# Backward pass of a linear-attention and SwiGLU block: the gradient of w2 computed transposed, with hh as the moving operand

## The chip, the cores and the metric

The kernel runs on one NeuronCore of a Trainium2 chip. A NeuronCore has five engines that run side by side and meet only at semaphores: TensorE (matrix multiply, PE in the profile), VectorE (DVE), ScalarE (ACT), GpSimd (POOL) and SyncE (SP), and 16 DMA engines that move data between HBM and the on-chip memory SBUF. A matmul takes a stationary operand (`lhsT`, at most 128 x 128, loaded into the array by a weight load, PEld in the profile) and streams a moving operand (`rhs`) through it; the result is summed in PSUM, whose banks hold 512 float32 values in each of 128 partitions. The metric is device time in microseconds (us).

## The reference

The program is one transformer block, forward and backward, on 2048 tokens of width D = 640: layernorm, linear attention with 32 heads of 20, a residual; then layernorm, a gated MLP with F = 1728 hidden columns, a residual. All arrays are bfloat16. The outputs are the block's output and the gradients of its input and of the five weights. The part that matters here:

```python
def _B_ref(x, w1, w3, w2):
    gate = jnp.einsum("bsd,df->bsf", x, w1)
    up = jnp.einsum("bsd,df->bsf", x, w3)
    h = _silu(gate) * up
    out = jnp.einsum("bsf,fd->bsd", h, w2)
    return out
...
h2 = h + _B_ref(_layernorm(h, axis=-1), B_w1, B_w3, B_w2)
...
_out, _vjp = jax.vjp(_f, A_x, A_wqkv, A_wo, B_w1, B_w3, B_w2)
_grads = _vjp(grad_out)
```

The gradient of w2, [1728, 640], is hidden^T times grad_out: for each hidden column f and each model column d, the sum over the 2048 tokens of h[s, f] x grad_out[s, d]. In the kernel it is `out_6`. The gradients of w1 and w3, [640, 1728] each, are `out_4` and `out_5`.

## The kernel before

The kernel is written with a manual schedule: the order of the code is the order of each engine's instructions, and of the DMA queues that SP, ACT and GpSimd issue into. The framework adds the waits: a reader waits for its writer, and a tile that takes over another's memory waits for its last user. `dma` is a copy issued from SP, `dmaT` a transposing load issued from SP, `dmaG` a copy issued from GpSimd, `A.dma_start` a copy issued from ACT. An engine that issues a DMA waits, in its queue, for what that DMA needs; what stands behind it waits too.

The stages in time (us from the start of the span):

1. Up to about 343: layernorms, the forward attention and the MLP. The MLP runs over four chunks of 512 tokens and 14 tiles of 128 hidden columns (the last has 64); the hidden activations are written to HBM transposed, as `hh_d` [F, S], and what the backward pass of w1 and w3 needs as `gg_d` [2F, S]. The last of it on TensorE is the down projection of the last chunk (`o2_steps`, lines 849 and 878).
2. 343 to 402, the gradient of w2 (lines 1033 to 1103). `load_hh` (line 1035) brings back `hh_d` with transposing loads, in four blocks of hidden columns of 512, 512, 512 and 192, as `hb[b]` [128 tokens of a tile, 16 tiles, columns]; block 0 comes in two loads of 256. Block 3 takes the buffer of block 0 (tags "ABCA"). `g2` holds grad_out by tokens. For each of 13 full tiles `fc` of 128 hidden columns, and each half j of D (320 columns), 16 matmuls sum over the token tiles: the stationary operand is 128 columns of hh, the moving operand 320 columns of `g2` (line 1089). ACT casts the two halves (line 1092), and issues the write of the 128 x 640 tile to `out_6` (line 1093). The last 64 hidden columns are `gw2_tail` (line 1070), called before the last full tile: 32 matmuls with a stationary operand of 64 columns, the two halves of D at two halves of the array. Between the tiles SP is given the loads that come next: block 3 of hh after fc 3, the transposed w1 and w3 (`load_w13`, line 1057) after fc 5, the first two pieces of `gg_d` (`load_gg`, line 1064) after fc 8 and 11.
3. 402 to 564: the gradient at the second layernorm (`b_ghn`, line 1126, with 27 x 2 matmuls a token tile), then the gradients through the output projection and the heads. The tile `g_h` [128, 16 token tiles, 640] is written here, and used up to the last token tile of stage 5.
4. 564 to 628: gradients of the attention's products, and of wqkv.
5. 628 to 702: the gradient at the first layernorm, by token tiles (`e_gxn`, line 1502). In it SP loads the first two blocks of `gg_d` (`load_block`, line 1478), again transposing, 496 columns of the 3456 (2F) a block, into two alternating buffers `gb`.
6. 702 to the end (lines 1540 to 1554): the gradients of w1 and w3. For each of seven blocks and each of five slices m of D, `grad_job` (line 1328) runs 16 matmuls with 128 columns of the normalized activations `hnN` as the stationary and up to 496 columns of `gb` as the moving operand (line 1338), with eight accumulators; ACT casts the result into `obs` (line 1342) and issues the write (line 1344), in halves for the first four jobs. SP first transposes the gradient of wo (kept in HBM as `dwoT_d`) into the first five tiles of `g_h`, which are free by then (line 1543), and writes it out (line 1544); then, after the jobs of block i, it loads block i + 2, whose buffer is block i's.

Of the kernel before, what the change touches and what calls it, by code (L numbers as in the profile page):

```python
# [9 lines left out]
P = 128  # L10
BF16 = mybir.dt.bfloat16
F32 = mybir.dt.float32
# [6 lines left out]
S, D, H, F = 2048, 640, 32, 1728  # L19
DH = D // H  # L20
ST, DT = S // P, D // P
FT, FP = 14, 1792
FL = F - 13 * P
W, SC, TPC = 512, 4, 4
HD = D // 2
NG = 27
# [29 lines left out]
def kernel(  # L56
# [19 lines left out]
    V, A, T, G, SY = nc.vector, nc.scalar, nc.tensor, nc.gpsimd, nc.sync  # L76
    dma, dmaT, dmaG = SY.dma_start, SY.dma_start_transpose, G.dma_start
# [12 lines left out]
    dram = ctx.enter_context(tc.tile_pool(name="dram", bufs=1, space=bass.MemoryType.DRAM))  # L90
# [5 lines left out]
    w_d = dram.tile([D, D], BF16, name="w_d")  # L96
    kvT_d = dram.tile([D, D], BF16, name="kvT_d")
    dwoT_d = dram.tile([D, D], BF16, name="dwoT_d")
    hn_d = dram.tile([S, D], BF16, name="hn_d")
    hh_d = dram.tile([F, S], BF16, name="hh_d")  # L100
    gg_d = dram.tile([2 * F, S], BF16, name="gg_d")
# [2 lines left out]
    def pool(name, side="left", space=None):  # L104
        kw = dict(space=space) if space is not None else dict(side=side)
        return tc.alloc_tile_pool(name=name, bufs=1, reuse_waits="tile", **kw)
# [71 lines left out]
    ps = pool("p1p", space=PSUM)  # L178
# [48 lines left out]
    def load_w13(c0, c1):  # L227
        def go1():
            dma(out=w1[:, c0:c1, 0:F], in_=rows(B_w1)[:, c0:c1, :])

        def go3():
            dma(out=w3[:, c0:c1, :], in_=rows(B_w3)[:, c0:c1, 0:F - FL])
        return [go1, go3]
# [18 lines left out]
    def p1_tr(t, parts=((0, DT),)):  # L252
        xn = x_sb[:, t, :]
        for a, b in parts:
            tr = ps.tile([P, DT, P], BF16, name="tr", bufs=2)
            for c in range(a, b):
                T.transpose(tr[:, c, :], xn[:, c * P:(c + 1) * P], ident[:])

            A.copy(out=pqT[:, a:b, t * P:(t + 1) * P], in_=tr[:, a:b, :])
# [13 lines left out]
    def p1_mm(t, n0, between=None, halves=None):  # L273
        acc = p1_acc() if halves is None else None
        for j in range(2):
            p1_half(acc[:, j, 0:HD] if halves is None else halves[j][:, 0:HD], t, n0 + j * HD)
            if j == 0 and between is not None:
                between()
        return acc
# [240 lines left out]
    for t in range(ST):  # L520
        first = None
        if t < RAW:
# [11 lines left out]
            k = p1_mm(t, D, between, kh)  # L534
            act(0, 1)
            act(1, 1)
        else:
            k = p1_mm(t, D, (lambda: p1_tr(t + 1)) if t + 1 < XT_DMA else None)
# [95 lines left out]
    ps = pool("pap", space=PSUM)  # L634
# [350 lines left out]
    for c in range(SC):  # L985
# [9 lines left out]
        for fc in range(FT):  # L995
# [8 lines left out]
            if c == 0 and fc in (5, 7, 9, 11):  # L1004
                a, b = {5: (0, 3), 7: (3, 6), 9: (6, 10), 11: (10, 13)}[fc]
# [10 lines left out]
            if c == SC - 1 and fc == 0:  # L1016
                g2 = U1.tile([P, ST, D], BF16, name="g2", tag="Q")
                tail = U2.tile([P, DT, P], BF16, name="w13tail", tag="g2T", bufs=2)
            if c == SC - 1 and fc in (1, 2, 5, 6):
                i = (1, 2, 5, 6).index(fc)  # L1020
# [9 lines left out]
    drain(1)  # L1030


    hb, blk = {}, [(0, 512), (512, 512), (1024, 512), (1536, 192)]

    def load_hh(b):
        f0, fw = blk[b]
        hb[b] = U2.tile([P, ST, 512], BF16, name="hb", tag="ABCA"[b])
        for a, n in ((0, 2 * P), (2 * P, 2 * P)) if b == 0 else ((0, fw),):
            dmaT(out=hb[b][:, :, a:a + n], in_=hh_d[f0 + a:f0 + a + n, :])

    load_hh(0)
    for _ in o2_steps(SC - 1, A.dma_start):
        drain(1)
# [6 lines left out]
    br = pool("br", "right")  # L1050
    ps = pool("pcp", space=PSUM)
    load_hh(1)
    load_hh(2)
    woT = U1.tile([P, DT, D], BF16, name="woT", tag="W6")
    kvN = br.tile([P, DT, D], BF16, name="kvN")
# [8 lines left out]
    def load_gg(j, c0, c1, q=dma):  # L1064
        if c0 == 0:
            ggb[j] = ba.tile([P, NG, 2 * P], BF16, name="ggb", bufs=2)
        q(out=ggb[j][:, c0:c1, :],
            in_=gg_d[c0 * P:c1 * P, j * 2 * P:(j + 1) * 2 * P].rearrange("(c p) w -> p c w", p=P))

    def gw2_tail():  # L1070

        gt = ps.tile([P, 2, 512], F32, name="gt", tag="gw", bufs=4)
        for t in range(ST):
            for j in range(2):
                T.matmul(gt[j * FL:(j + 1) * FL, 0, 0:HD], lhsT=hb[3][:, t, P:P + FL],
                         rhs=g2[:, t, j * HD:(j + 1) * HD], start=(t == 0), stop=(t == ST - 1))
        ob = br.tile([P, HD], BF16, name="gts")
        A.copy(out=ob[:], in_=gt[:, 0, 0:HD])
        for j in range(2):
            A.dma_start(out=out_6[F - FL:F, j * HD:(j + 1) * HD], in_=ob[j * FL:(j + 1) * FL, :])  # L1080

    for fc in range(FT - 1):
        b, i = divmod(fc, 4)
        if fc == FT - 2:
            gw2_tail()
        acc = ps.tile([P, 2, 512], F32, name="gw", bufs=4)
        for j in range(2):
            for t in range(ST):
                T.matmul(acc[:, j, 0:HD], lhsT=hb[b][:, t, i * P:(i + 1) * P], rhs=g2[:, t, j * HD:(j + 1) * HD],  # L1089
                         start=(t == 0), stop=(t == ST - 1))  # L1090
        ob = br.tile([P, D], BF16, name="gw2o", bufs=2)
        A.copy(out=ob[:].rearrange("p (j n) -> p j n", j=2), in_=acc[:, :, 0:HD])
        A.dma_start(out=out_6[fc * P:(fc + 1) * P, :], in_=ob[:])
        if fc == 3:
            load_hh(3)
        if fc == 5:
            load_w13()
        if fc == 8:
            load_gg(0, 0, NG)
        if fc == 11:  # L1100
            load_gg(1, 0, NG)
    ps.release()
    U2.release()

# [4 lines left out]
    g_h, g_n = g_hx[:, :, G0:G0 + D], g_hx[:, :, G0 + D:]  # L1109
# [4 lines left out]
    ps = pool("pbp", space=PSUM)  # L1114
# [134 lines left out]
    for t in range(ST):  # L1249
# [14 lines left out]
        if t >= 1:  # L1264
# [3 lines left out]
            if t <= 2 * DT:  # L1268
                n = (t - 1) % DT
# [24 lines left out]
    a, b = ST - 1, ST - 2  # L1294
# [33 lines left out]
    def grad_job(lhs, m, rhs, n, out, q=dma):  # L1328
        for _ in grad_halves(lhs, m, rhs, n, out, q):
            pass  # L1330
# [30 lines left out]
    ps = pool("pdp", space=PSUM)  # L1361
# [3 lines left out]
    def d_acc():  # L1365
        return ps.tile([P, 2, 512], F32, name="dkv", bufs=3)

    def square(lhsT, rhs, i):

        acc = d_acc()  # L1370
        for c, a, b, bank, off, first in SQ:
            T.matmul(acc[:, bank, off:off + (b - a) * DH], lhsT=lhsT[:, c, i * P:(i + 1) * P],
                     rhs=rhs[:, c, a * DH:b * DH], start=first, stop=True, skip_group_check=True)
        return acc
# [12 lines left out]
    for m, (a, b) in enumerate(M_H):  # L1387
        n = (b - a) * DH
        acc = ps.tile([P, 512], F32, name="gkvT", tag="dkv", bufs=3)
        for c in range(DT):  # L1390
            T.matmul(acc[:, 0:n], lhsT=woT[:, c, m * P:(m + 1) * P], rhs=QT[:, c, a * DH:b * DH], start=(c == 0),
                     stop=(c == DT - 1))
# [38 lines left out]
    acc = d_acc()  # L1431
    for m in range(DT):
        T.matmul(acc[:, m // 4, m % 4 * P:(m % 4 + 1) * P], lhsT=ones[:], rhs=gzd[:, m, :], start=(m % 4 == 0),
                 stop=True, skip_group_check=True)
# [3 lines left out]
    for t in range(ST):  # L1438
        c, i = divmod(t, TPC)
        u = t // 2  # L1440
        acc = d_acc()
        for j in range(2):
            for k in range(DT):
                T.matmul(acc[:, j, 0:HD], lhsT=xnT[c][:, k, i * P:(i + 1) * P], rhs=gm[:, k, j * HD:(j + 1) * HD],  # L1444
                         start=(k == 0), stop=(k == DT - 1))
# [7 lines left out]
        if t in (2, 5, 8, 11, 14):  # L1453
            n = t // 3
            acc = square(mN, gkv_b, n)
            k = (4, 0, 1, 2, 3)[n]
            ob = obs[:, k * D:(k + 1) * D]
# [6 lines left out]
        if t in (6, 8, 10, 12):  # L1464
            n = t // 2 - 3
# [12 lines left out]
    def load_block(i, a=0, b=NB):  # L1478
        if i < len(blocks):
            f0, f1 = blocks[i]  # L1480
            if a == 0:
                gb[i] = ex.tile([P, ST, NB], BF16, name="gb", bufs=2)
            b = min(b, f1 - f0)
            dmaT(out=gb[i][:, :, a:b], in_=gg_d[f0 + a:f0 + b, :])

    def both_grads(m, f0, f1):

        return [(max(f0, lo) - f0, min(f1, lo + F) - f0, out[:, m, max(f0, lo) - lo:min(f1, lo + F) - lo])
                for lo, out in ((0, out4S), (F, out5S)) if max(f0, lo) < min(f1, lo + F)]
# [24 lines left out]
    ps = pool("pep", space=PSUM)  # L1514
# [26 lines left out]
    ps = pool("pfp", space=PSUM)  # L1541
    njob = 8
    dmaT(out=g_h[:, 0:DT, :], in_=dwoT_d[:, :])
    dma(out=out3S, in_=g_h[:, 0:DT, :])
    for i, (f0, f1) in enumerate(blocks):
        n = f1 - f0
        for m in range(DT):
            last = (i, m) == (len(blocks) - 1, DT - 1)
            for a, b in ((0, n - P), (n - P, n)) if last else ((0, n),):
                c = (a + b) // 2  # L1550
                halves = ((a, c), (c, b)) if i * DT + m < 4 else ((a, b),)
                out = [(x + y - a, z + y - a, to) for y, w in halves for x, z, to in both_grads(m, f0 + y, f0 + w)]
                grad_job(hnN, m, lambda t: gb[i][:, t, a:b], b - a, out, A.dma_start)
        load_block(i + 2)
    ps.release()
    ex.release()
    bv.release()
# [33 lines left out]
```

## Time and profile before

| | |
|---|---|
| median of the 3 runs shown | 822.33 us (821.93 to 822.73) |
| the profiled execution | 823.24 us, of which the span is 821.5 |
| mean granted clock of TensorE | 0.999 of full speed |
| ScalarE, VectorE, GpSimd busy | 39%, 55%, 16% of the span |
| stage 2, the matmuls of line 1089 | 416 of 128x320, weights 128 x 128 |
| stage 2, the casts of line 1092 | 13, 692 ns each |
| stage 2, writes of `out_6` from ACT | 13 of 160 KB, 5.7 us to land (median), and 2 of 40 KB |
| stage 2, loads of hh | 5, 6.9 to 13.4 us to land |
| stage 6, loads of `gb` | 9, 4.8 to 12.3 us to land |
| stage 6, casts of 496 columns | 30, 571 ns each |

How to read it. The span is the time from the first to the last instruction of one profiled execution; the execution's own time has 1.74 us more around it. Times of lines are microseconds from the span's start. The busy time of a matmul overlaps that of the next, so what a stream of matmuls costs is read from the chain of work in order of time, where a piece has a start, a length, a line and a count. Lines marked SPq or ACTq are the instructions that issue DMAs: their length is the time the issuing took; "to landing" counts from the start of the issue until the data is there. In the page's second part each digit is the busy share of a fortieth of the span, in tenths.

### The profile page before, as it was taken

What the parts mean: (1) busy time and instruction counts of PE and PEld (TensorE: products, weight loads), DVE (VectorE), ACT (ScalarE), POOL (GpSimd) and SP (SyncE); (2) the same over time, 40 slices, a digit from 0 to 9 for tenths busy, and PEclk for the clock granted to TensorE, in tenths of its full rate; (3) what the DMA queues carried; (4) which work ended last, traced back from release to release, by engine and by line L of the source; (5) the groups of instructions that cost most, each with busy time, mean ns of one, the idle gap of its engine ahead of it and who ended that gap; (6) DMA issues with size and microseconds to landing.
All of it is one profiled execution on the core that took longest, in us unless ns stands there. A gap on an engine that the chain in (4) does not pass through costs nothing.

```text
span 821.5 us, 13988 instructions
## 1 busy us (share of the span) xinstructions
PE 812.4 (99%) x5427; PEld 513.4 (62%) x5454; DVE 453.0 (55%) x975; ACT 323.2 (39%) x603; POOL 130.8 (16%) x193
## 2 busy tenths in 40 slices
PE   8999999999999999999999999999999999999998
PEld 5677544555555545777777777777777777544444
DVE  7859897999898566400057777772681545200000
ACT  6866687655655666011121212222212334211111
POOL 2234343333323212100001111110220000000000
PEclk9999999999999999999999999999999999999999
DMA  9899989796485556999878897259995797968651
GB/s 248 225 284 229 201 235 286 240 241 165 131 218 158 153 195 168 222 260 249 236 167 183 200 209 191 68 112 178 260 225 93 178 190 165 234 164 184 165 139 36
DMA packets 323745, 157.88 MB, mean 192 GB/s; under 512 B 242528, under 2 KB 316928, under 8 KB 323680
## 3 DMA queue, kind: packets, MB, share of 16 engines
q1 hardware_dynamic: 281056, 116.18, 61.9%
q0 software_dynamic: 7328, 24.48, 8.7%
q10 hardware_dynamic: 35296, 16.34, 8.6%
q8 instruction: 42, 0.69, 0.4%
q14 instruction: 23, 0.19, 0.1%
HBM read 47.09 MB, written 51.13 MB: 120 GB/s over the span
## 4 chain that ended last, share of the span: by engine, by line
PE 96%; DMA 2%; SPq 1%; ACT 0%; DVE 0%; issue 0%
PE mm L387 20%; PE job L1338 19%; PE ghn L1134 14%; PE gxn L1507 8%; PE gw L1089 7%; PE o L903 4%; PE big L267 4%; PE o L849 3%; PE gwo L1222 3%; PE macc L422 3%; PE gr L1191 3%; PE dkv L1444 3%; PE at L647 2%; PE mm L267 1%; DMA g2T<-in_grad_out_dram 1%; DMA pqT<-pql 1%
## 5 line engine op out<-in xcount | busy, mean ns | idle before, releaser
L1338 PE MATMUL job<-gb,hnN 128*128 128x496 bf16 (+3 forms) x576 | 116.8, 366 | 0.0
L1134 PEld LDWEIGHTS <-ggb 128*128 128x128 bf16 x864 | 84.5, 98 | 32.8
L387 PE MATMUL mm<-pqT,w 128*128 128x512 bf16 x396 | 93.3, 379 | 0.9 <-ACT up L793 0.2
L1338 PEld LDWEIGHTS <-hnN 128*128 128x128 bf16 x576 | 55.8, 98 | 61.0
L387 PEld LDWEIGHTS <-w 128*128 128x128 bf16 x540 | 52.7, 98 | 63.6 <-issue 1.4
L1342 ACT CAST obs<-job 128x496 bf16<-128x496 f32 (+4 forms) x56 | 28.5, 509 | 123.7 <-PE job L1338 120.9
L1134 PE MATMUL ghn<-w13a,ggb 128*128 128x320 bf16 x448 | 63.5, 299 | 0.0
L1149 DVE SCALAR_TENSOR_TENSOR wb<-gs,hnb 128x640 f32<-128x640 bf16 x16 | 13.2, 825 | 89.4 <-ACT gs L1146 89.4
L1134 PE MATMUL ghn<-w13b,ggb 128*128 128x320 bf16 x416 | 61.4, 299 | 0.0
L387 PE MATMUL mm<-g2T,w2T 128*128 128x512 bf16 x228 | 58.8, 379 | 0.6
L1089 PE MATMUL gw<-g,hb 128*128 128x320 bf16 x416 | 56.8, 299 | 0.0
L1199 POOL TENSOR_TENSOR sz<-Zb,g_h 128x640 f32<-128x640 bf16 x16 | 20.2, 1260 | 197.7 <-DVE g_h L1200 197.7
L1089 PEld LDWEIGHTS <-hb 128*128 128x128 bf16 x416 | 40.6, 98 | 16.0 <-issue 0.3
L412 ACT CAST ghh<-mm 128x512 bf16<-128x512 f32 x48 | 28.1, 586 | 49.9 <-PE mm L387 41.2
L786 ACT ACTIVATE sig<-mm 128x512 bf16<-128x512 f32 x56 | 33.8, 603 | 24.3 <-PE mm L387 20.6
L1146 ACT ACTIVATE gs<-ghn 128x640 bf16<-128x640 f32 x16 | 11.2, 703 | 78.8 <-PE ghn L1134 78.8
L387 PEld LDWEIGHTS <-w2T 128*128 128x128 bf16 x260 | 25.4, 98 | 24.6 <-issue 1.2
L267 PEld LDWEIGHTS <-pqT 128*128 128x128 bf16 x320 | 30.6, 98 | 14.0 <-issue 1.3
L267 PE MATMUL big<-wqkv,pqT 128*128 128x320 bf16 x250 | 38.4, 299 | 0.2
L822 DVE TENSOR_TENSOR gate<-gate,sig 128x1024 bf16<-128x1024 bf16 x28 | 19.3, 689 | 34.4 <-ACT gate L797 31.6
L1338 PEld LDWEIGHTS <-g 128*128 128x128 bf16 x320 | 31.0, 98 | 11.6
L903 PE MATMUL o<-w,hhT 128*128 128x320 bf16 x224 | 35.0, 299 | 0.0
(216 smaller groups left out, 1368.7 us busy)
## 6 DMA issues: line engine op xcount, KB each, us to landing
hh_d<-hhT SPq DMA_DIRECT2D x24, 256.0 KB, 2.6
gg_d<-gate POOLq DMA_DIRECT2D x24, 256.0 KB, 4.1
gg_d<-ghh POOLq DMA_DIRECT2D x24, 256.0 KB, 4.1
ggb<-gg_d SPq DMA_DIRECT2D x6, 896.0 KB, 5.3
ggb<-gg_d ACTq DMA_DIRECT2D x6, 832.0 KB, 6.3
x_sb<-in_A_x_dram SPq DMA_DIRECT2D x6, 640.0 KB, 5.8
ggb<-gg_d SPq DMA_DIRECT2D x2, 1728.0 KB, 13.2
out_dram<-obs ACTq DMA_DIRECT2D x21, 124.0 KB, 3.1
```

The costliest lines, as they stand in the source:

```text
L267: T.matmul(acc, lhsT=pqT[:, c, t * P:(t + 1) * P], rhs=wqkv[:, c, n0:n0 + HD], start=(c == 0), stop=(c == DT - 1))
L387: T.matmul(acc[:], lhsT=w[:, c, fc * P:(fc + 1) * P], rhs=rhs[:, c, :], start=(c == 0), stop=(c == DT - 1))
L412: A.copy(out=ghh[n // 2][:, n % 2, :], in_=acc[:])
L422: T.matmul(macc[m][j][:, 0:n], lhsT=pk_all[:, t, m * P:(m + 1) * P], rhs=x_ext[:, t, j * HD:j * HD + n], start=(t == 0), stop=(t == ST - 1))
L786: A.activation(sig[:, i, :], gp[:], AF.Sigmoid)
L849: T.matmul(accs[i, j][:, 0:HD], lhsT=hhT[c][:, fc, i * P:(i + 1) * P], rhs=w2[:, fc, j * HD:(j + 1) * HD], start=(first and fc == 0), stop ...
L903: T.matmul(o2["ps"][:, 0:HD], lhsT=hhT[c][:, fc, i * P:(i + 1) * P], rhs=w2[:, fc, j * HD:(j + 1) * HD], start=(fc == 0), stop=(fc == FT - 1))
L1089: T.matmul(acc[:, j, 0:HD], lhsT=hb[b][:, t, i * P:(i + 1) * P], rhs=g2[:, t, j * HD:(j + 1) * HD], start=(t == 0), stop=(t == ST - 1))
L1134: T.matmul(acc[:, j, 0:HD], lhsT=ggb[t // 2][:, k, lo:lo + P], rhs=rhs[:, j * HD:(j + 1) * HD], start=(k == 0), stop=(k == NG - 1))
L1338: T.matmul(acc[:, 0:n], lhsT=lhs[:, t, m * P:(m + 1) * P], rhs=rhs(t), start=(t == 0), stop=(t == ST - 1))
L1342: A.copy(out=ob, in_=acc[:, 0:n])
L1507: T.matmul(acc[:, j, 0:HD], lhsT=g, rhs=wqT[:, k, j * HD:(j + 1) * HD], start=(k == 0), stop=(k == 14))
```

## The change

The gradient of w2 is computed as its transpose, [640, 1728]. For each block of hidden columns, now 256, 512, 512 and 448 wide, and each of the five slices of 128 columns of D, 16 matmuls have the slice of `g2` as the stationary and the whole block of hh as the moving operand. The separate tail is gone. A result is one PSUM bank (eight of them instead of four pairs); ACT casts it into one of three buffers and writes it to a new array in HBM, `gw2T_d` [640, 1792]; the last block is padded to 512 columns with zeros by GpSimd. The loads that were issued between the tiles are issued after the blocks: block 3 of hh after block 0, w1 and w3 after block 1, the pieces of `gg_d` after blocks 2 and 3. Block 0 is loaded by one transposing load of 256 columns.

In the last stage SP issues four transposing loads of `gw2T_d` into free tiles of `g_h` (tiles 5 and 6, 7 to 10, 11 to 14, and 0 to 3 once the gradient of wo has been written out from there), two before the jobs of block 0 and two behind the load of block 2; and, behind the load of block 3, the five copies from there to `out_6`. The first seven jobs instead of four write their results in halves.

```diff
+    gw2T_d = dram.tile([D, FP], BF16, name="gw2T_d")
...
-    hb, blk = {}, [(0, 512), (512, 512), (1024, 512), (1536, 192)]
+    hb, blk = {}, [(0, 256), (256, 512), (768, 512), (1280, 448)]
 
     def load_hh(b):
         f0, fw = blk[b]
         hb[b] = U2.tile([P, ST, 512], BF16, name="hb", tag="ABCA"[b])
-        for a, n in ((0, 2 * P), (2 * P, 2 * P)) if b == 0 else ((0, fw),):
-            dmaT(out=hb[b][:, :, a:a + n], in_=hh_d[f0 + a:f0 + a + n, :])
+        dmaT(out=hb[b][:, :, 0:fw], in_=hh_d[f0:f0 + fw, :])
...
-    def gw2_tail():
-
-        gt = ps.tile([P, 2, 512], F32, name="gt", tag="gw", bufs=4)
-        for t in range(ST):
-            for j in range(2):
-                T.matmul(gt[j * FL:(j + 1) * FL, 0, 0:HD], lhsT=hb[3][:, t, P:P + FL],
-                         rhs=g2[:, t, j * HD:(j + 1) * HD], start=(t == 0), stop=(t == ST - 1))
-        ob = br.tile([P, HD], BF16, name="gts")
-        A.copy(out=ob[:], in_=gt[:, 0, 0:HD])
-        for j in range(2):
-            A.dma_start(out=out_6[F - FL:F, j * HD:(j + 1) * HD], in_=ob[j * FL:(j + 1) * FL, :])
-
-    for fc in range(FT - 1):
-        b, i = divmod(fc, 4)
-        if fc == FT - 2:
-            gw2_tail()
-        acc = ps.tile([P, 2, 512], F32, name="gw", bufs=4)
-        for j in range(2):
+    for b, (f0, fw) in enumerate(blk):
+        for m in range(DT):
+            acc = ps.tile([P, 512], F32, name="gw", bufs=8)
             for t in range(ST):
-                T.matmul(acc[:, j, 0:HD], lhsT=hb[b][:, t, i * P:(i + 1) * P], rhs=g2[:, t, j * HD:(j + 1) * HD],
-                         start=(t == 0), stop=(t == ST - 1))
-        ob = br.tile([P, D], BF16, name="gw2o", bufs=2)
-        A.copy(out=ob[:].rearrange("p (j n) -> p j n", j=2), in_=acc[:, :, 0:HD])
-        A.dma_start(out=out_6[fc * P:(fc + 1) * P, :], in_=ob[:])
-        if fc == 3:
+                T.matmul(acc[:, 0:fw], lhsT=g2[:, t, m * P:(m + 1) * P], rhs=hb[b][:, t, 0:fw], start=(t == 0),
+                         stop=(t == ST - 1))
+            ob, fp = br.tile([P, 512], BF16, name="gw2o", bufs=3), (fw + P - 1) // P * P
+            if fp > fw:
+                G.memset(ob[:, fw:fp], 0.0)
+            A.copy(out=ob[:, 0:fw], in_=acc[:, 0:fw])
+            A.dma_start(out=gw2T_d[m * P:(m + 1) * P, f0:f0 + fp], in_=ob[:, 0:fp])
+        if b == 0:
             load_hh(3)
-        if fc == 5:
+        if b == 1:
             load_w13()
-        if fc == 8:
-            load_gg(0, 0, NG)
-        if fc == 11:
-            load_gg(1, 0, NG)
+        if b > 1:
+            load_gg(b - 2, 0, NG)
...
     dmaT(out=g_h[:, 0:DT, :], in_=dwoT_d[:, :])
     dma(out=out3S, in_=g_h[:, 0:DT, :])
+    turned = [DT, DT + 2, DT + 6, 0]
+
+    def gw2_turn(b):
+        f0, fw = blk[b]
+        n = (fw + P - 1) // P
+        dmaT(out=g_h[:, turned[b]:turned[b] + n, :], in_=gw2T_d[:, f0:f0 + n * P])
+
+    def gw2_out(b):
+        f0, fw = blk[b]
+        n, k = fw // P, turned[b]
+        dma(out=out_6[f0:f0 + n * P, :].rearrange("(k p) d -> p k d", p=P), in_=g_h[:, k:k + n, :])
+        if fw % P:
+            dma(out=out_6[f0 + n * P:f0 + fw, :], in_=g_h[0:fw % P, k + n, :])
+
+    for b in range(2):
+        gw2_turn(b)
     for i, (f0, f1) in enumerate(blocks):
...
-                halves = ((a, c), (c, b)) if i * DT + m < 4 else ((a, b),)
+                halves = ((a, c), (c, b)) if i * DT + m < 7 else ((a, b),)
...
         load_block(i + 2)
+        if i == 0:
+            gw2_turn(2)
+            gw2_turn(3)
+        if i == 1:
+            for b in range(4):
+                gw2_out(b)
```

## The prediction, made before the change was run

> **What bounds the kernel now.** I read the page's shares first, then the chain of work that ended last in order of time, then the queue on SP (the engine that issues nearly all loads) in the two stages the change touches. From the page (slices are 20.5 us each):
>
> ```profile
> span 821.5 us, 13988 instructions
> PE 812.4 (99%) x5427; PEld 513.4 (62%) x5454; DVE 453.0 (55%) x975; ACT 323.2 (39%) x603; POOL 130.8 (16%) x193
> DMA  9899989796485556999878897259995797968651
> ```
>
> TensorE is busy 99% of the span, so only fewer or cheaper matmuls, or a shorter tail, can make the kernel faster, and any new wait of TensorE makes it slower by its whole length. DMA is near full in the changed stage (slices 17 to 20) and less full in the last one (35 to 40). The chain in order of time (start, length, what):
>
> ```profile
> 293.46 6.47 PE mm L387 x30
> ...
> 342.88 52.16 PE gw L1089 x384
> 395.04 2.29 PE gt L1075 x32
> 397.34 4.45 PE gw L1089 x32
> 401.79 19.56 PE ghn L1134 x144
> ...
> 568.25 1.56 PE gkvT L1391 x25
> ...
> 701.84 116.65 PE job L1338 x576
> ```
>
> The gradient of w2 is the piece from 342.88 to 401.79, 58.91 us, with no wait inside it or at its ends. The last stage is 116.65 us of matmuls, also unbroken. So both stages are bound by the stream of matmuls, and the loads are hidden. The question is whether they stay hidden.
>
> **What the matmuls cost.** A busy figure of one matmul overlaps its neighbours, so I take spacings from the chain: 52.16/384 = 135.83 ns for 320 columns, 6.47/30 = 215.67 ns for 512 (line 387). That is 0.4158 ns a column and 2.76 ns fixed. A test: 496 columns give 209.0 ns, and a block of the last stage takes (735.34 - 718.61)/80 = 209.1 ns. Before: 416 of 320 columns, plus 32 tail matmuls that run two at a time, 58.91 us in sum. After: 80 matmuls (5 slices of D, 16 token tiles) of 256, 512, 512 and 448 columns: 80 x (109.2 + 215.67 + 215.67 + 189.05) ns = 58.37 us. The columns streamed are the same (13 x 2 x 16 x 320, with half of 32 x 320 for the tail, is 138,240, as is 80 x 1728). What is saved is the fixed part of 128 matmuls and the tail's pairs: **0.54 us**. The 256-column width has no row. The 140-column row (line 1391) takes 62.4 ns where the formula gives 61.0, with a new weight load for each, so 256 columns cost 109.2 to 110.6 ns: at most 0.1 us for the 80. I take the low end, as 320 columns lie nearer.
>
> The Trainium skill, "TensorE: Matmul & The Clock Gate", section "Back-to-back issue gap", gives sustained spacings of about 131 ns at 512 columns and 81 at 128, and says that the columns-plus-fixed formula counts too much at large widths. By a line through its two figures the stage would be about 9 us shorter, an estimate from that page. This trace has 215.67 ns at 512 columns, so I don't use it.
>
> **ScalarE, GpSimd and the stage's end.** 13 casts of 692 ns and one of 425 become 20, of 256 to 512 columns (586 ns is the row for 512). Groups end every 1.75 us at the soonest. A write of 160 KB took 5.7 us to land; with three output buffers a cast in the 256-column block may wait up to 5.7 - 3 x 1.75 = 0.5 us. Behind it in ACT's queue stand only this stage's casts and writes, and TensorE has eight accumulators (14 us of work in that block), so it waits for none. The five small memsets are on GpSimd, which has nothing between 335 and 410. The next stage takes over banks whose casts are long done, save the last, which it needs only at its second tile 8.7 us later. All this: nothing. Without that cover, 0.5 us a cast.
>
> The Trainium skill, "DMA: Bandwidth & Descriptors", section "Bandwidth", calls transfers under 64 KB dominated by their descriptors; that speaks against pieces of 64 KB as the first block writes. Here 62 KB writes from ACT took 3.1 us in the median and 124 KB ones 3.0 to 3.2 in the same busy stretch, so halving brings nothing back. By the rule the five first writes would cost as much as large ones; nobody waits for them.
>
> **The loads of hh, the tight place.** SP in the changed stage:
>
> ```profile
> 331.85 33.91 SPq L1039 DMA_TRANSPOSE hb<-hh_d  x5
> 365.81 9.18 SPq L1058 DMA_TRANSPOSE w13a<-in_B_w_dram  x1
> 375.21 10.41 SPq L1059 DMA_TRANSPOSE w13b<-in_B_w_dram  x1
> 387.25 4.63 SPq L1067 DMA_DIRECT2D ggb<-gg_d  x2
> ```
>
> It issues one load behind the other. Asked one by one, the hb loads land like this (rows of hh; issue; landing): 256 at 331.85 and 340.65; 256 at 336.88 and 346.9; 512 at 343.39 and 354.5; 512 at 351.90 and 365.3; 192 at 362.14 and 369.0. After, the pieces are 256, 512, 512, 448, the same 1728 rows. The first lands as before. The second is needed when the 256-column block is done: 342.88 + 80 x 0.1092 = 351.62. Before, 512 rows had landed by 346.9 and 1024 by 354.5, so 768 are there at about 350.7; ACT's 64 KB writes begin at 344.6 instead of 348 and may add 0.3. It is in time by 0.6 to 0.9 us. Bounds: issued at 336.88 and as quick as the 343.39 load, 11.1 us, it lands at 348.0; the 6.51 us issue of the second 256 rows, then a whole 10.0 us issue and 3.8 us to land, give 357.2. I take 351, nearest to the row counts. Each us past 351.62 is a us of TensorE. The third piece is due at 368.9 (1280 rows at about 360), the fourth at 386.1 (1728 at about 369, its buffer free at 351.6). Behind them, the first ggb load landed at 397.35 (10.1 us after issue) and is due at 401.25: 3.9 us of cover, against 0.3 us for 0.08 MB more written and perhaps 0.7 for narrower rows.
>
> **The last stage.** SP there (the next lines, then the load of block 3 with its landing):
>
> ```profile
> 698.45 7.93 SPq L1484 DMA_TRANSPOSE gb<-gg_d  x1
> ...
> 707.55 3.94 SPq L1543 DMA_TRANSPOSE g_h<-dwoT_d  x1
> 715.43 0.38 SPq L1544 DMA_DIRECT2D out_dram<-g_h  x1
> ```
> ```profile
> L1484 SPq DMA_TRANSPOSE gb<-gg_d x1: 9127/9127/9127, 735.3 to 735.3; - x1
> DMA to landing us min/median/max: 12.3/12.3/12.3
> ```
>
> Turning 640x640 elements took SP 3.94 us, 9.6 ns per 1000; so the first two turns (640x256, 640x512) take 1.58 + 3.15 us, from 715.81 to 720.54. The load of block 2, issued at 718.61 before, goes 1.9 us later; it took 10.1 us to land (block 3's: 12.3), so it lands at 730.6 to 732.8 and is due at 735.34. The turns' 0.98 MB, at the 290 GB/s seen in full stretches, is 3.4 us of DMA; if all of it came on top, 736.2. Turns 3 and 4 (6.3 us) are behind block 2 on SP, and end by about 736.0; block 3's load starts up to 0.7 us late and lands by 748.3, due at 752.08. The five output writes stand behind that load and wait for turns that have landed by then; block 4's load waits for TensorE until 752.08 anyway. Three more jobs with halved output writes add 3 issues of 0.34 us to ACT, with eight accumulators of 3.35 us between it and TensorE. So nothing on the path; without the cover, block 2 costs what it is late. The end (last cast and write) is the same.
>
> **Sum.** The profiled execution took 823.24 us, 821.5 of span and 1.74 around it; less 0.54 is 822.70. It lies 0.91 above the median shown, 822.33, so the median goes to 821.79: **821.8 us**, 0.07% less. A measurement of this kernel tells about 0.2% (1.64 us) from no change, so this is no change.
>
> **Rivals.**
> 1. *The second hh piece is late* (the slower side). For it: SP and the DMA engines are full from 332 on, and 0.6 us is little; the engines also fell idle for about a us at 342 and 360. Against: both row counting and the 11.1 us row put it in time. Landing up to 353.8 hides within 0.2%; from there the kernel is slower, to 821.8 + 5.6 = 827.4 at the far bound. Small form (0.3 to 2 us late): 822.1 to 823.8, 0.20; large form, some 825: 0.05.
> 2. *Block 2's load is late behind the turns.* For it: the turns stand ahead of it on SP. Against: 2.5 us of cover at the slower row. Price 0.9 us: 822.7, 0.08; if also slowed by output writes beyond any row here, some 825: 0.04.
> 3. *The change doesn't shorten the matmuls*, as 256 columns or full banks cost more than the formula: up to 0.54 back, 822.3; 0.07. Against: 512 and 496 columns fit.
> 4. *Faster beyond 0.2%* needs 1.64 us, and TensorE has no wait in either stage to lose: 0.02.
>
> The forecast itself has 0.52, and 0.02 is left for what I do not see.
>
> **How the numbers follow.** Faster 0.02; slower 0.05 + 0.04 + 0.02 (unseen) = 0.11; within 0.2%: 0.87. The range goes from 821.2 (the runs before spread 0.4 either way, and the page's rounding) to 823.8, the end of rival 1's small form; outside lie the large forms.
>
> **What would show it.** Right: matmuls at 109, 216 and 189 ns, the stage 58.4 us long, the next one starting near 401.3, the last stage unbroken at 116.65. Wrong: a gap of TensorE at 351.6 ended by an hb load (rival 1), at 735 ended by a gb load (rival 2), or 512-column spacing off 215.7.

## The result, and the profile after

The changed kernel takes 824.62 us in the median (823.34 to 825.89, 10 runs), the kernel before 822.13 (821.57 to 823.36, 10 runs): a ratio of 1.0026, 95% interval 1.0018 to 1.0034. It is slower by some 2.5 us, where 0.5 us less was forecast. (The ratios and intervals in this document are those on record; they aren't quotients of the medians, 1.0030 here, and differ from them by up to 0.0009.) The profiled execution took 823.93 us, with a span of 822.0.

From the page of the changed kernel, the lines that answer to the first ones of before:

```profile
span 822.0 us, 13808 instructions
PE 813.2 (99%) x5326; PEld 501.7 (61%) x5326; DVE 453.0 (55%) x975; ACT 325.0 (40%) x609; POOL 131.6 (16%) x198
DMA  9999889796485555999767787259995897999951
```

The page looks the same: 99% of TensorE, ScalarE at 40% instead of 39%. A loss of 2 us in 822 can't be seen in shares. The list of what TensorE waited for shows it at once (line waited for: us in total, times, longest):

```profile
PE ghn L1119 <- ACT gw2o L1079: 1.8, 1, 1.8
PE gw L1074 <- DMA hb<-hh_d: 0.5, 1, 0.5
```

Neither line is in the list of before. The first says that the stage after the w2 gradient (`ghn`) began 1.8 us late, because of a cast of ScalarE; the second is the second piece of hh. The chain of work through the changed stage (start, length, what) shows how a cast comes to be that late:

```profile
335.70 15.08 DMA hb<-hh_d
...
350.82 22.70 PE gw L1074 x105
373.52 13.68 DMA w13b<-in_B_w_dram
...
387.28 0.34 ACTq L1080
...
387.71 0.59 ACT gw2o L1079
...
388.33 5.47 DMA gw2T_d<-gw2o
...
395.39 5.89 DMA gw2T_d<-gw2o
...
401.42 0.16 POOL gw2o L1078
...
401.82 0.54 ACT gw2o L1079
...
402.41 19.72 PE ghn L1119 x144
```

From 373.5 on it isn't matmuls that set the time: a load of w3 (`w13b`) lands at 387.20, and only then does ScalarE issue a write of a w2-gradient tile, which has nothing to do with w3; then casts and writes follow one another, each cast behind the write that frees its buffer (5.5 to 5.9 us to land), up to the last cast at 402.36. ScalarE by itself around that point (start, length, what; idle before and its releaser in brackets):

```profile
371.74 0.59 ACT L1079 CAST gw2o<-gw 128x512 bf16<-128x512 f32 x1 [2.87 <-PE gw L1074]
376.36 0.34 ACTq L1080 DMA_DIRECT2D gw2T_d<-gw2o  x1
...
378.65 0.59 ACT L1079 CAST gw2o<-gw 128x512 bf16<-128x512 f32 x1 [1.27 <-PE gw L1074]
387.28 0.34 ACTq L1080 DMA_DIRECT2D gw2T_d<-gw2o  x1
387.71 0.59 ACT L1079 CAST gw2o<-gw 128x512 bf16<-128x512 f32 x1 [8.48 <-DMA w13b<-in_B_w_dram]
```

The cast at 378.65 is done at 379.24, its write is issued 8 us later. Two facts of the built program explain the two halves of this. **The write:** the framework gives each DMA that SP or ACT issues one of eight completion counters, in turn over both queues, and lets the issue wait until the counter's last DMA has landed. The trace bears this out: eight semaphores take turns there, and a write's wait names the semaphore of an earlier load. The writes of this stage share counters with the big loads: the write at 350.86 waits for the second piece of hh (landed 350.8), that of 359.93 for the third, that of 376.36 for w1, that of 387.28 for w3. All stand in ScalarE's queue, and the casts behind them wait too. **The bank:** the eight accumulators are laid on banks 0, 7, 6, 1, 2, 3, 4, 5 in turn (the profile shows no banks; e1 below shows what they do). The twentieth and last lies in bank 1, and the first tile of `ghn` takes banks 0 and 1; so its first matmul waits for the last cast. Before, the last accumulator lay in the pair from bank 6, and `ghn`'s first tile took over only what the tail had used: it began ahead of the last cast (start, length, what):

```profile
401.63 1.11 PE L1134 MATMUL ghn<-w13a,ggb 128*128 128x320 bf16 x7
401.83 0.69 ACT L1092 CAST gw2o<-gw 128x640 bf16<-128x640 f32 x1 [4.02 <-PE gw L1089]
```

The last stage is still unbroken (116.65 us from 702.62), but with nothing to spare. SP's queue there (start, length, what; the "turns" are the transposing loads of `gw2T_d`, line 1535):

```profile
708.49 4.46 SPq L1528 DMA_TRANSPOSE g_h<-dwoT_d  x1
716.85 0.38 SPq L1529 DMA_DIRECT2D out_dram<-g_h  x1
717.28 6.21 SPq L1535 DMA_TRANSPOSE g_h<-gw2T_d  x2
723.59 8.87 SPq L1469 DMA_TRANSPOSE gb<-gg_d  x1
```

Block 2 of `gb` is issued at 723.59, 4.2 us after its buffer came free (80 matmuls of 209.1 ns after 702.62, 719.35), and took 12.2 us: it landed at 735.8, and was due at 736.08.

The sum of the profiled executions: from the first matmul of the w2 gradient (342.72 before, 341.45 after) to where the chain puts the start of `ghn` (401.79 and 402.41), 59.07 became 60.96, +1.89; `ghn`'s first 144 matmuls, which start from an empty pipeline, took 19.72 instead of 19.56, +0.16. That is 2.05 of the 2.5 us; the rest isn't located (the profiled execution was 0.7 us under the median). Up to the stage the code is the same, and the stage's start varies by over a microsecond from one execution to the next, which is why the two spans differ by only 0.5.

### The profile page after: what moved, and what is told of

It is laid out like the page before. It is cut to its first block, busy times and chain, and to the rows that moved or that the text cites. A ratio compares the mean times of both kernels' runs of the same rounds, so it can differ in the third digit from the quotient of the medians.

```text
span 822.0 us, 13808 instructions
## 1 busy us (share of the span) xinstructions
PE 813.2 (99%) x5326; PEld 501.7 (61%) x5326; DVE 453.0 (55%) x975; ACT 325.0 (40%) x609; POOL 131.6 (16%) x198
## 4 chain that ended last, share of the span: by engine, by line
PE 91%; DMA 7%; ACT 1%; DVE 1%; SPq 0%; issue 0%; ACTq 0%; POOL 0%; POOLq 0%; DVEq 0%
PE mm L388 20%; PE job L1323 19%; PE ghn L1119 14%; PE gxn L1492 8%; PE o L904 4%; PE big L268 3%; PE gw L1074 3%; PE gwo L1207 3%; PE gr L1176 3%; PE dkv L1429 3%; PE o L850 3%; PE macc L423 2%; PE at L648 2%; DMA hb<-hh_d 2%; DMA w13b<-in_B_w_dram 2%; DMA gw2T_d<-gw2o 1%
## 5 line engine op out<-in xcount | busy, mean ns | idle before, releaser
L1074 PE MATMUL gw<-hb,g 128*128 128x512 bf16 (+2 forms) x320 | 58.7, 346 | 0.5 <-DMA hb<-hh_d 0.5
L1074 PEld LDWEIGHTS <-g 128*128 128x128 bf16 x320 | 31.3, 98 | 27.6 <-issue 0.7
L1323 PEld LDWEIGHTS <-g 128*128 128x128 bf16 x320 | 31.0, 98 | 11.6
L1079 ACT CAST gw2o<-gw 128x512 bf16<-128x512 f32 (+2 forms) x20 | 10.4, 519 | 65.4 <-PE gw L1074 28.0
```

The costliest lines, as they stand in the source:

```text
L1074: T.matmul(acc[:, 0:fw], lhsT=g2[:, t, m * P:(m + 1) * P], rhs=hb[b][:, t, 0:fw], start=(t == 0), stop=(t == ST - 1))
L1323: T.matmul(acc[:, 0:n], lhsT=lhs[:, t, m * P:(m + 1) * P], rhs=rhs(t), start=(t == 0), stop=(t == ST - 1))
```

## The experiments

Theories: **A**, the late last cast at the stage's end carries the loss; **B**, the load of block 2 behind the turns in the last stage carries it; **C**, the second piece of hh, or something else. The runs were made on three chips, each against the kernel before on the same chip (822.75, 822.77 and 822.20 us); e1 to e4, e5 to e8, and e9 with e10 share one each. The changed kernel itself was run again only beside e6 to e8 (e5); which chip the result came from isn't on record.

**e1, seven banks.** The last accumulator then lies in bank 3, away from `ghn`'s first tile.

```diff
-            acc = ps.tile([P, 512], F32, name="gw", bufs=8)
+            acc = ps.tile([P, 512], F32, name="gw", bufs=7)
```

> Seven accumulators for the transposed gradient instead of eight, nothing else: the last group then does not sit in the two PSUM banks that the next stage's first tile takes, so that tile needs cast 18 of 20 and not cast 20. Theory A (the loss is TensorE's wait for the last, late cast at the end of the stage, 1.8 us in the profile of the changed kernel): no gap between the last gw matmul and the first ghn matmul, and 1.5 to 2 us less than the changed kernel, 822.6 to 823.1 or a ratio of 1.0005 to 1.0012 to before. Theory B (the loss is in the last stage, block 2 of gb late behind the turning loads): the gap at the stage's end goes, but the time stays near 824.6, ratio 1.0026. Theory C (the late second piece of hh is the loss): also 1.0026, with a gap near 350 us that is larger than 1.5 us.

Measured: 824.0 us, ratio 1.002 (1.0009 to 1.003). Its chain:

```profile
351.45 49.83 PE gw L1074 x240
401.28 19.56 PE ghn L1119 x144
...
701.37 22.46 PE job L1323 x107
723.83 12.66 DMA gb<-gg_d
...
736.54 83.36 PE job L1323 x416
```

The first wait is gone: `ghn` starts at 401.28, where the matmuls end. Yet the last cast is later than in after (401.82), 3.2 us after `ghn` has begun:

```profile
404.44 0.53 ACT L1079 CAST gw2o<-gw 128x448 bf16<-128x448 f32 x1 [0.51 <-POOL gw2o L1078]
```

So the bank makes the wait, and not the late cast alone. But TensorE now reaches the last stage 1.25 us earlier, while SP issues block 2 no earlier (723.83; 723.59 in after), and TensorE waits 1.5 us there. In this profile the time won at the first place is mostly lost at the second. A isn't the whole; B's wait was hidden in the profile of after.

**e2, six output buffers**, so that a cast doesn't wait for the write three before it.

```diff
-            ob, fp = br.tile([P, 512], BF16, name="gw2o", bufs=3), (fw + P - 1) // P * P
+            ob, fp = br.tile([P, 512], BF16, name="gw2o", bufs=6), (fw + P - 1) // P * P
```

> Six output buffers instead of three for the casts, banks as in the changed kernel. Theory A in the form that the casts are late because each waits for the write of three casts before: the gap at the stage's end falls from 1.8 to about 0.6 us (one cast of 0.53 us), ratio about 1.0011. Theory A in the form that ACT's queue stands still because its writes wait for a long load from SP that used the same completion counter before: write 19 still waits for the second ggb load to land (401.1 us in the profile of the changed kernel) and the last cast stands behind it, so the gap stays at 1.0 to 1.8 us and the ratio at 1.0016 to 1.0026. Theory B: 1.0026 either way.

Measured: 827.45 us, 1.0059 (1.0042 to 1.0077): not better. The chain at the stage's end:

```profile
385.73 15.42 DMA ggb<-gg_d
...
401.25 0.34 ACTq L1080
...
401.69 0.54 ACT gw2o L1079
...
402.27 21.39 PE ghn L1119 x144
```

More buffers don't help: the write before the last cast shares a counter with a load of `ggb` and is issued when that lands, at 401.15 (in the profile of after it landed at 401.29, not at the 401.1 expected above, and the write that frees the last cast's buffer landed within 0.01 us of it, so there both held the cast). The wait is 2.8 us in this profile. And the 144 matmuls take 21.39 us, not 19.7: see the clock below.

**e3, the writes from GpSimd's queue**, with six buffers. GpSimd's DMAs have counters of their own.

```diff
-            A.dma_start(out=gw2T_d[m * P:(m + 1) * P, f0:f0 + fp], in_=ob[:, 0:fp])
+            dmaG(out=gw2T_d[m * P:(m + 1) * P, f0:f0 + fp], in_=ob[:, 0:fp])
```

> The 20 writes are issued by GpSimd instead of ACT, with six buffers; banks as in the changed kernel. GpSimd's DMAs have counters of their own, so ACT only casts. Theory A, counter form: every cast follows its matmuls at once, the gap at the stage's end is one cast, 0.6 us, and the ratio about 1.0011. If casts are still 1 us and more late, it is the landing of the writes that holds them. Theory B: 1.0026.

Measured: 825.17 us, 1.0036 (1.0023 to 1.0049). What TensorE waited for:

```profile
PE job L1323 <- DMA gb<-gg_d: 2.7, 1, 2.7
PE gw L1074 <- DMA hb<-hh_d: 0.8, 1, 0.8
PE ghn L1119 <- ACT gw2o L1079: 0.7, 1, 0.7
```

The wait at the stage's end is now one prompt cast of 0.54 us and its signals, as the counters would have it. In the last stage TensorE waits 2.7 us for block 2, and so neither theory's ratio came out.

**e4, no turns and no writes to `out_6`** (the gradient of w2 is left out of the outputs), eight banks.

> The changed kernel without the four turning loads and the five copies of the last stage (the gradient of w2 is left out of the outputs); everything before is as in the changed kernel. Theory A: the last stage had no loss to give back, so 824.3 to 824.7, ratio 1.0024 to 1.0027, at most 0.3 us better. Theory B: 1.5 to 2.5 us less than the changed kernel, ratio 1.0000 to 1.0008.

Measured: 827.61 us, 1.0053 (1.004 to 1.0066). The last stage is unbroken (116.66 us), so block 2 is in time without the turns; but the wait at the stage's end is 2.1 us here. The windows after it (us, PE busy, ..., granted clock, DMA share, GB/s):

```profile
404.00:406.00 2.00, 1.37 (x9) 0.94 (x9) 0.00 (x0) 0.53 (x1) 0.00 (x0) 0.90 0.70 207
406.00:408.00 2.00, 2.00 (x10) 1.08 (x8) 0.00 (x0) 0.00 (x0) 0.00 (x0) 0.50 0.79 253
408.00:410.00 2.00, 2.00 (x13) 1.26 (x12) 0.00 (x0) 0.00 (x0) 0.00 (x0) 0.75 0.00 1
```

The granted clock fell to half for some 3.4 us (the three rows lose 0.2, 1.0 and 0.5 us of clock, 1.7 together, which is half of 3.4). A kernel with less work came out above the result's ratio, which neither theory expected. Whether the missing turns have a part in that, this run can't say: no run of the changed kernel stands beside it on its chip. e5, on another chip, shows that the changed kernel itself can come out as high.

**e5, the changed kernel again**, beside e6 to e8.

> The changed kernel itself again, on the chip of the next three, as their control. Profile so far: 1.8 us wait at the stage's end (the first matmul of ghn, for the last cast of the w2 gradient), 0.5 us for the second piece of hh, 0.2 us for block 2 of gb in the last stage; 0.54 us gained by the matmuls. Theory A (the late last cast) and theory B (block 2 behind the turns) both expect a ratio to the kernel before of 1.002 to 1.003, as in the result (1.0026). If it is nearer 1.005, as the run without the turns was, that run's excess lay in the chip and its clock, not in the missing turns. The sum of waits less 0.54 should explain the runs at full clock: +1.9 us, 1.0023.

Measured: 828.12 us, 1.0065 (1.0047 to 1.0083). From its waits, and its chain:

```profile
PE job L1323 <- DMA gb<-gg_d: 2.4, 1, 2.4
PE ghn L1119 <- ACT gw2o L1079: 2.0, 1, 2.0
PE gw L1074 <- DMA hb<-hh_d: 0.6, 1, 0.6
```
```profile
739.52 85.05 PE job L1323 x416
```

The changed kernel has no fixed loss: both waits stand at the edge where a few tenths more cost another 1.7 us of clock (85.05 instead of 83.36 for the same 416 matmuls). Here 3 of 6 executions had a mean clock of 0.998, in the result 1 of 10.

**e6, the turns behind the loads of `gb`**, eight banks:

```diff
-    for b in range(2):
-        gw2_turn(b)
...
         load_block(i + 2)
-        if i == 0:
-            gw2_turn(2)
-            gw2_turn(3)
-        if i == 1:
+        if i < 4:
+            gw2_turn(i)
+        if i == 4:
             for b in range(4):
                 gw2_out(b)
```

> Only the turns move: each goes behind a load of gb (block 2, 3, 4, 5), and the writes to out_6 behind block 6. Theory A: the wait at the stage's end stays, 1.8 us, so the time stays at 1.0015 to 1.0026. Theory B (the turns ahead of block 2 carry most of the loss): the loss goes, 0.999 to 1.0005. Both expect no wait for block 2 in the last stage: SP issues it when block 0's jobs end, as in the kernel before.

Measured: 825.88 us, 1.0033 (1.002 to 1.0047), against 1.0065 for e5 on the same chip. SP's queue, then the wait that is left:

```profile
721.82 0.39 SPq L1529 DMA_DIRECT2D out_dram<-g_h  x1
723.81 8.58 SPq L1469 DMA_TRANSPOSE gb<-gg_d  x1
732.44 1.40 SPq L1535 DMA_TRANSPOSE g_h<-gw2T_d  x1
```
```profile
PE ghn L1119 <- ACT gw2o L1079: 3.8, 1, 3.8
```

Block 2 is issued when TensorE is done with its buffer (707.05 + 80 x 0.2091 = 723.78), and the last stage is unbroken. About half of the loss is gone (the two intervals just meet, at 1.0047). B alone is out (it expected all of it to go), and so is A alone, by which the turns would be worth nothing. In the profiled execution, 0.3 for hh, 3.8 for the cast and 1.8 for the clock and the refilling of the pipeline after it, less 0.54, make 5.4 us; that execution took 828.11, 5.3 above the median of before.

**e7, seven banks and the turns moved** (e1 and e6 together).

> Seven accumulator banks instead of eight, and the turns behind the gb loads. If the two waits are the whole loss (theories A and B together): only the second piece of hh (0.3 to 0.8 us) is left against the 0.54 us that the matmuls gain, so 0.0 to +0.3 us, 0.9998 to 1.0006, and both waits are gone from the profile. Rival C (the loss lies in something else: more writes and DMAs in general, or the second piece of hh being much later in most executions): it stays at 1.0015 or more though the two waits are gone.

Measured: 822.78 us, 1.0001 (0.999 to 1.0013). Waits, and chain:

```profile
PE gw L1074 <- DMA hb<-hh_d: 0.4, 1, 0.4
```
```profile
350.37 49.83 PE gw L1074 x240
400.19 19.56 PE ghn L1119 x144
...
700.25 116.65 PE job L1323 x576
```

Both waits are gone, and so is the loss. Rival C is out: writing the gradient through HBM and turning it costs nothing that can be measured, to within about 1 us.

**e8, the wait for the second piece of hh taken away too:** the turns as in e7, but hh in five pieces of 256, 256, 512, 512 and 192 columns, and the banks kept apart by giving the last block three accumulators of its own; the loads between the blocks are moved to match.

```diff
-    hb, blk = {}, [(0, 256), (256, 512), (768, 512), (1280, 448)]
+    hb, blk = {}, [(0, 256), (256, 256), (512, 512), (1024, 512), (1536, 192)]
...
-            acc = ps.tile([P, 512], F32, name="gw", bufs=8)
+            acc = ps.tile([P, 512], F32, name="gw", tag="gx" if b == 4 else "gw", bufs=3 if b == 4 else 5)
```

> As the kernel before it, with the banks kept apart in another way (the last block's accumulators have three banks of their own, the others five), and hh in five pieces of 256, 256, 512, 512 and 192 columns, loaded as the kernel before loads it: the matmuls of the second piece then wait only for 256 rows. 16 matmuls a slice more (400 instead of 320) cost 80 x 2.76 ns = 0.22 us, so the stage gains 0.3 us instead of 0.54. If the second piece of hh costs 0.3 to 0.8 us in the other runs, it is gone here: -0.3 us, 0.9994 to 1.0002. If the loss lies elsewhere (rival C), it stays at 1.0015 or more.

Measured: 822.48 us, 0.9997 (0.9987 to 1.0007): no difference from before. The wait for the second piece is gone (0.4 us remain before the first), but the last block, with three accumulators for its five results, makes TensorE wait 0.8 us for a cast inside the stage (398.78, ahead of the last 32 of its matmuls), the same standing queue in another place.

**e9, e3 with the turns moved:** eight banks, so that `ghn` still begins in the bank of the last cast, but the casts are prompt.

> Eight accumulator banks as in the change, so that the next stage still begins in the bank of the last cast; but the 20 writes go through GpSimd's queue, with six buffers, so that no cast stands behind a write; and the turns go behind the gb loads, so that block 2 is in time. Theory A1 (the shared bank costs only because the last cast is late, and it is late because ACT's queue stands behind its writes): the wait of ghn is one cast, 0.6 to 0.7 us, the hh piece 0.3 to 0.8, less 0.54: +0.4 to +1.0 us, 1.0003 to 1.0013, clock undisturbed. Theory A2 (a shared bank costs about 2 us however prompt the cast is): the wait is 1.8 us or more, 1.002 to 1.0035.

Measured: 823.41 us, 1.0015 (1.0004 to 1.0026). Waits:

```profile
PE gw L1074 <- DMA hb<-hh_d: 0.8, 1, 0.8
PE ghn L1119 <- ACT gw2o L1079: 0.7, 1, 0.7
```

The shared bank costs one cast, 0.7 us, when the cast is prompt (A1). The time alone lies between the two expectations, and its interval reaches into both; the wait decides.

**e10, seven banks, no turns, no `out_6`** (the gradient of w2 left out of the outputs).

> Seven accumulator banks, and neither the turns nor the writes to out_6 (the gradient of w2 stays in HBM, transposed, and is left out of the outputs). If turning the gradient in the last stage is wholly hidden once it stands behind the gb loads, this takes the same time as the kernel with seven banks and the turns moved (1.0001): 0.9993 to 1.0008, with the last stage unbroken at 116.65 us. If the turns also cost something else there (slower loads, a longer end), it is under that by more than 0.001. It also tells whether the run without the turns and with eight banks (1.0053) was slow by the stage's end alone.

Measured: 822.04 us, 1.0007 (0.9994 to 1.002), last stage 116.66 us: the same as e7 within the intervals. With the bank clash gone, leaving the turns out gains nothing that can be measured, so moved turns are hidden; and e4's loss lay at the stage's end.

All profiles together (us of TensorE's waits; "halved" is a fall of the granted clock after a wait):

| | hh piece | stage's end | block 2 | halved after | ratio |
|---|---|---|---|---|---|
| after | 0.5 | 1.8 | under 0.2 | none | 1.0026 |
| e1 seven banks | 0.3 | 0 | 1.5 | none | 1.002 |
| e2 six buffers | 0.4 | 2.8 | 1.4 | 2.8 | 1.0059 |
| e3 GpSimd's queue | 0.8 | 0.7 | 2.7 | 2.7 | 1.0036 |
| e4 no turns | 0.6 | 2.1 | 0 | 2.1 | 1.0053 |
| e5 after, again | 0.6 | 2.0 | 2.4 | 2.4 | 1.0065 |
| e6 turns moved | 0.3 | 3.8 | 0 | 3.8 | 1.0033 |
| e7 both | 0.4 | 0 | 0 | none | 1.0001 |
| e8 five pieces | 0.4 (the first piece) | 0 (0.8 inside the stage) | 0 | none | 0.9997 |
| e9 e3, turns moved | 0.8 | 0.7 | 0 | none | 1.0015 |
| e10 e7 without turns | 0.8 | 0 | 0 | none | 1.0007 |

## Why the prediction was wrong, point by point

- **The matmuls: right.** The 80 of 256 columns took 8.90 us, of which the last is 0.27: (8.90 - 0.27)/79 = 109.2 ns, as forecast. The last 240 took 49.83 us; the formula gives 49.63. In the profiles without a wait at the end (e1, e7, e10), first matmul to first matmul of `ghn` (by the same two points as above) is 59.0, 59.1 and 59.5 us; less the hh wait, 58.72 in each, against 59.07 before: 0.35 us gained, not 0.54. What is missing is about one refill of the pipeline after the hh wait (0.27 - 0.11 us). Rival 3 is out. (The 9 us that the prediction estimates from the skill's two figures count the tail's 32 matmuls one by one; as pairs, as in its own sum, it would be 7. The forecast didn't use it.)
- **"ScalarE, GpSimd and the stage's end ... All this: nothing": the step that failed.** "The next stage takes over banks whose casts are long done, save the last, which it needs only at its second tile 8.7 us later" was argued from the old layout of the banks; in the new one the last cast is the first thing it needs (e1 takes the wait away by the bank alone, with a cast that is later still). And "Behind it in ACT's queue stand only this stage's casts and writes" looked at what stands behind, not at what a write itself waits for: I allowed 0.5 us, and writes stood up to 8 us behind loads (387.28). Before has the same rule without harm: its write at 388.52 also came just after w3's landing, 1.4 us after its cast. Casts that are late cost nothing while eight accumulators lie between; the twentieth has none behind it. The size: 1.8 to 3.8 us, and 1.7 more where the clock fell.
- **The last stage: "So nothing on the path" failed by its margin.** I let SP reach block 2 at 720.54, 18.7 us after the stage's start; it was 21.0. The writing out of wo's gradient came 0.6 us later in the stage, and the two turns took 6.21 us to issue, not 4.73. The price was right for each by itself: in e6, each behind a load of `gb`, they took 1.40 and 3.35 us; why they took longer one behind the other isn't shown. The landing, 12.2 us, was in my 10.1 to 12.3. So 2.3 us of the 2.5 us of cover were gone at once. In e1, e2, e3 and e5 SP issued block 2 22.4 to 22.9 us after the stage's start and it took 12.4 to 13.3 us to land, 1.4 to 2.7 us late. This was rival 2, given 0.12; its price of 0.9 us was too small, and the fall of the clock behind such a wait (1.7 us in e3 and e5) was in no price: the prediction counted a wait of TensorE at its own length.
- **The second hh piece: rival 1 in its small form**, 0.3 to 0.8 us in all profiles but e8's (in after it landed at 350.8, near the forecast 351, while the stage began 1.3 us earlier than in the profile of before). By itself it would have left the time within the range.
- **The turns and copies as such: right.** Moved behind the loads they are hidden (e7 against e10).
- **What no step had:** that two rivals can be true together, and that removing one wait brings the other out (after to e1).

Still open: why the same kernel loses 2.5 us in the result and 5.3 in e5. The waits of e5 were only some tenths longer at the stage's end and 2.2 us longer at block 2, and the clock explains 1.7 us. Block 2 was issued 22.5 us after the stage's start instead of 21.0, and took 13.3 us to land instead of 12.2; why was not tried.

## What to carry to other kernels

Where a stage ends, look up which banks and buffers the next one takes first, and who used them last: here eight accumulators hid a late cast everywhere except at the hand-over. A write that shares a set of completion counters with large loads can be as late as those loads, so its queue should hold nothing that TensorE will want soon. And when a stage has two covers that are nearly used up, undo both in one run: with one undone, much of the loss was left (1.002 and 1.0033); with both undone it was gone (1.0001).

## What the runs showed of the hardware

A short wait of TensorE can cost nearly twice its length. In these profiles waits of up to 2.0 us were followed by a full clock (after, e1, and e5 at the stage's end: 19.72 us for `ghn`'s first 144 matmuls); waits of 2.1 us and more (e2, e3, e4, e5 at block 2, e6) by a granted clock of 0.5 for about 3.4 us, which cost 1.7 us: 21.38 or 21.39 us for the same 144, 85.05 instead of 83.36 for 416 in the last stage. Five waits are too few to call 2.1 us a fixed edge. All executions together fit: a mean clock of 0.998 or less stood in 4 of 5 of e4, 3 of 6 of e2 and of e5, 1 of 6 of e3 and of e6, 2 of 12 of e1 and 1 of 10 of the result, and in none of the 47 of e7 to e10, whose profiles have no wait over 0.8 us in these stages.

The Trainium skill, "TensorE: Matmul & The Clock Gate", section "What's actually happening", lets the clock fall to half after at least one idle window of about 3.4 us that runs free of the kernel. The half clock did last about that long here, but the fall came after waits that were shorter; the measurement decides, and here a wait under 3.4 us was not safe.

The Trainium skill, "Perfetto Trace Analysis", section "Matmuls", advises to rotate groups of matmuls through different banks, so that the emptying of one overlaps the next. Inside the stage that held: no wait for a cast with seven or eight banks in turn, 0.8 us in the block with three (e8). Where the rotation ends it was not enough: with eight banks, and the writes in ScalarE's queue, the last cast cost 1.8 to 3.8 us.
